# Channel gate over a 384x384x384 image: tiles of 60 rows in four slots instead of 44 rows in six, and a shorter first load

## The chip, the cores and the metric

The kernel runs on one core of a Trainium2 chip. The metric is the device time of one execution in microseconds (us). It is about 1.6 us longer than the span of the profile, which runs from the first to the last instruction.

PE is TensorE, DVE is VectorE, ACT is ScalarE, SP is SyncE, POOL is GpSimd. "Engine" alone means a compute engine; the 16 DMA engines are always called so.

## The reference, cut to what matters

```python
g = jnp.einsum("bhwc->bc", x) / (H * W)      # mean of each of 384 channels
s = sigmoid(g * w1d[0])                      # k = 1: one weight
return x * s[:, None, None, :]               # x is (1, 384, 384, 384), bfloat16
```

The gate depends on all of x, and x (113.25 MB) doesn't fit on the chip. Read plainly, this needs x twice and the output once. The kernel avoids the second reading by a guess that it checks, as follows.

## The kernel before: the parts that matter

A "row" here is 384 channels of one pixel in each of 128 partitions, 98,304 bytes; x has 1152 such rows. The kernel computes an early gate `s_early` from the first 4 rows, multiplies every tile by it and stores it, while PE sums all rows. In the end it compares the true gate with the early one, bit by bit, and would do everything again if they differed. With these inputs they agree, and that second pass isn't run.

```python
FIRST, EARLY, TILE, SLOTS, BOTH = 8, 4, 44, 6, 4
...
load(base, FIRST, 0)                              # 8 lead rows, SyncE's queue
for k in range(BOTH):                             # first tiles: half on each queue
    load(slot(k), TILE, row0(k), ("sync", "scalar"))
    if k == 0:
        plan.dma("scalar", w_one[0:1, 0:1], w1d.unsqueeze(0), writes=["w_one"])
for k in range(BOTH, SLOTS):
    load(slot(k), TILE, row0(k))                  # the others on SyncE's queue
...
for k in range(n_tiles):
    if k >= SLOTS:
        put(slot(k), TILE, row0(k - SLOTS))       # multiply in place, then store
        load(slot(k), TILE, row0(k))              # waits until that store has landed
    there = rows(slot(k), TILE)
    plan.relay(ready, "gpsimd", "tensor", there, there, ["acc1"])   # PE sums the tile
plan.signals("tensor", rows(base, FIRST), ["acc1"])
for k in range(n_tiles - SLOTS, n_tiles):
    put(slot(k), TILE, row0(k))
put(base, FIRST, 0)                               # the lead rows are stored last
```

`put` is one DVE multiply over the whole tile and one store on ScalarE's queue. The planner derives the waits: the multiply writes the tile in place, so it waits until PE has summed it. A tile's way is therefore load, landing, PE sum, DVE multiply, store, landing, and then its slot is free for another load.

## Time and profile before

| | before |
|---|---|
| device time, median | 529.16 us (529.02 to 529.28, 4 runs) |
| span of the profile | 527.6 us |
| moved by DMA | 226.53 MB, 429 GB/s |
| PE, DVE busy | 46% each |

The page of the kernel before: busy time of the engines, the DMA engines' share of each of 40 slices in tenths, and the packets.

```profile
PE 243.7 (46%) x851; PEld 0.2 (0%) x2; DVE 241.1 (46%) x45; ACT 2.7 (1%) x4; POOL 0.3 (0%) x6
...
DMA  9999999999999999999999999999999999999998
...
DMA packets 8357, 226.53 MB, mean 429 GB/s; under 512 B 930, under 2 KB 930, under 8 KB 1186
```

The 16 DMA engines are the bound: no slice but the last is below nine tenths. The Trainium skill, "DMA: Bandwidth & Descriptors", Where 436 GB/s comes from, puts the ceiling of 16 ports at 435.2 GB/s; full stretches of this trace show 433.

The chain of waits of the same kernel; its last piece (start, us, what) is the check of the guess:

```profile
515.11 0.15 DVE redo L415
```

This chain isn't what ends the run. The packet records go on until 527.1 us. The chain follows instructions, and the last stores have no instruction after them, so in a DMA-bound kernel the tail must be read from the DMA records.

The tail of the kernel before, in order of time (start us, length us, engine, line, operation, and in brackets the idle time before it and what ended it):

```profile
488.75 22.25 ACTq L109 DMA_DIRECT2D out_dram<-arena  x3
490.56 4.00 PE L238 MATMUL acc<-arena,ones 128*128 128x512 bf16 x9 [10.84 <-PEq L279]
494.78 5.19 PE L238 MATMUL acc<-arena,ones 128*128 128x512 bf16 x23 [0.22 <-issue]
...
500.01 10.63 DVE L202 TENSOR_TENSOR arena<-arena,s_early 128x16896 bf16<-128x16896 bf16 x2 [11.29 <-PE acc L238]
```

The last load landed at 489.9 us. PE summed that tile until 500.0; the first 9 matmuls took 4.00 us and the next 23 took 5.19, which fits what the Trainium skill, "TensorE: Matmul & The Clock Gate", Part 1, says of a clock that is at half speed after idling. DVE multiplied the tile (8.96 us) and then the 8 lead rows (1.75 us). The store of the tile was issued at 509.0 us.

The stretches around it (us; busy time and number of instructions of PE, PEld, DVE, ACT, POOL; granted clock; DMA share; GB/s). A packet is counted whole in the stretch in which it starts, so a share may pass 1:

```profile
500.00:505.00 5.00, 0.62 (x3) 0.00 (x0) 4.99 (x1) 0.00 (x0) 0.00 (x0) 1.00 1.00 433
505.00:510.00 5.00, 0.00 (x0) 0.00 (x0) 5.00 (x2) 0.00 (x0) 0.00 (x0) 0.51 1.02 439
510.00:515.00 5.00, 0.00 (x0) 0.00 (x0) 4.11 (x9) 0.61 (x1) 0.00 (x0) 0.50 0.99 426
515.00:520.00 5.00, 0.00 (x0) 0.00 (x0) 0.22 (x2) 0.00 (x0) 0.00 (x0) 0.50 1.00 433
```

By the packet records the first DMA engine ended the earlier stores at 513.6 us, and the last tile's packets followed at once.

DMA issues (output<-input, queue, count, KB each, median us from issue to landing), and the making of the early gate:

```profile
out_dram<-arena ACTq DMA_DIRECT2D x26, 4224.0 KB, 52.7
arena<-in_x_dram SPq DMA_DIRECT2D x22, 4224.0 KB, 48.1
```

```profile
12.60 0.16 PE L337 MATMUL w_all<-w_one,ones 1*128 1x1 bf16 x1 [12.60 <-DMA w_one<-in_w1d_dram]
...
16.93 0.61 ACT L369 ACTIVATE s_early<-total,w_scaled 128x384 bf16<-128x384 f32 x1 [12.55 <-DVE total L311]
...
26.24 17.83 DVE L202 TENSOR_TENSOR arena<-arena,s_early 128x16896 bf16<-128x16896 bf16 x2 [9.35 <-PE acc L238]
```

The gate was ready at 17.5 us, but the first multiply began at 26.24, when PE had summed the first tile. The gate wasn't what it waited for.

### The profile page before, as it was taken

What the parts mean: (1) busy time and instruction counts of PE and PEld (TensorE: products, weight loads), DVE (VectorE), ACT (ScalarE), POOL (GpSimd) and SP (SyncE); (2) the same over time, 40 slices, a digit from 0 to 9 for tenths busy, and PEclk for the clock granted to TensorE, in tenths of its full rate; (3) what the DMA queues carried; (4) which work ended last, traced back from release to release, by engine and by line L of the source; (5) the groups of instructions that cost most, each with busy time, mean ns of one, the idle gap of its engine ahead of it and who ended that gap; (6) DMA issues with size and microseconds to landing.
All of it is one profiled execution on the core that took longest, in us unless ns stands there. A gap on an engine that the chain in (4) does not pass through costs nothing. (4 is left out here: it accounts for less than half of the span.)

```text
span 527.6 us, 1093 instructions
## 1 busy us (share of the span) xinstructions
PE 243.7 (46%) x851; PEld 0.2 (0%) x2; DVE 241.1 (46%) x45; ACT 2.7 (1%) x4; POOL 0.3 (0%) x6
## 2 busy tenths in 40 slices
PE   0876561652651651652742642642733733633700
PEld 0000000000000000000000000000000000000000
DVE  0298626326336336336246336246156156156190
ACT  1000000000000000000000000000000000000000
POOL 0000000000000000000000000000000000000000
PEclk9998867866767867866757867868757768768765
DMA  9999999999999999999999999999999999999998
GB/s 384 430 429 410 428 438 436 425 446 418 443 425 441 436 425 446 418 443 420 446 433 428 443 420 443 420 446 433 428 443 420 441 423 443 436 425 446 416 443 358
DMA packets 8357, 226.53 MB, mean 429 GB/s; under 512 B 930, under 2 KB 930, under 8 KB 1186
## 3 DMA queue, kind: packets, MB, share of 16 engines
q10 hardware_dynamic: 4466, 121.90, 53.6%
q1 hardware_dynamic: 3888, 104.60, 46.2%
q8 instruction: 1, 0.02, 0.0%
q14 instruction: 2, 0.02, 0.0%
HBM read 113.25 MB, written 113.25 MB: 429 GB/s over the span
## 5 line engine op out<-in xcount | busy, mean ns | idle before, releaser
L238 PE MATMUL acc<-arena,ones 128*128 128x512 bf16 x846 | 242.6, 453 | 244.3 <-PEq L279 242.7
L202 DVE TENSOR_TENSOR arena<-arena,s_early 128x16896 bf16<-128x16896 bf16 (+1 forms) x27 | 234.5, 8691 | 259.2 <-PE acc L238 259.2
L337 PE MATMUL w_all<-w_one,ones 1*128 1x1 bf16 x1 | 0.2, 158 | 12.6 <-DMA w_one<-in_w1d_dram 12.6
L346 DVE TENSOR_SCALAR w_scaled<-w_all 128x1 f32<-128x1 f32 x2 | 0.2, 154 | 11.6 <-PE w_all L337 11.6
L311 DVE TENSOR_TENSOR total<-total,acc 128x128 f32<-128x128 f32 (+2 forms) x11 | 4.5, 408 | 0.3
L393 ACT ACTIVATE arena<-total,w_scaled 128x384 bf16<-128x384 f32 x1 | 0.6, 615 | 495.7 <-DVE total L311 495.7
L331 ACT ACT_TABLE_LOAD x1 | 1.3, 1283 | 2.9 <-issue 2.9
L309 DVE COPY total<-acc 128x384 f32<-128x384 f32 x1 | 0.6, 558 | 1.2 <-PE acc L238 1.2
L401 DVE TENSOR_TENSOR total<-arena,s_early 128x384 f32<-128x384 uint16 x1 | 0.6, 559 | 0.7 <-ACT arena L393 0.7
L238 PE MATMUL acc<-zeros,ones 128*128 128x512 bf16 x3 | 0.8, 380 | 0.0
L369 ACT ACTIVATE s_early<-total,w_scaled 128x384 bf16<-128x384 f32 x1 | 0.6, 615 | 12.5 <-DVE total L311 12.5
L355 DVE MEMSET ones<- 128x128 bf16 x1 | 0.2, 165 | 1.0 <-PEq L522 1.0
L236 PE MATMUL acc<-arena,ones 128*128 128x512 bf16 x1 | 0.6, 607 | 0.0
L409 DVE TENSOR_REDUCE wrong<-total 128x1 f32<-128x384 f32 x1 | 0.6, 553 | 0.0
L331 ACT ACTIVATE warm<-warm 128x1 f32<-128x1 f32 x1 | 0.2, 203 | 0.0
L415 DVE CAST redo<-wrong 128x1 int32<-128x1 f32 x1 | 0.2, 153 | 0.0
L236 PEld LDWEIGHTS acc<-arena,ones 128*128 128x128 bf16 x1 | 0.1, 106 | 0.0
L337 PEld LDWEIGHTS w_all<-w_one,ones 1*128 1x128 bf16 x1 | 0.1, 100 | 12.6 <-issue 12.6
L522 POOL MEMSET const-bfloat16-1.0<- 128x1 bf16 x1 | 0.1, 101 | 0.0
L522 POOL MEMSET const-uint8-127<- 128x1 uint8 x1 | 0.1, 101 | 0.0
L354 POOL MEMSET zeros<- 128x2 bf16 x1 | 0.1, 99 | 0.0
L353 POOL MEMSET warm<- 128x1 f32 x1 | 0.1, 98 | 0.5 <-POOLq L522 0.5
(2 smaller groups left out, 0.2 us busy)
## 6 DMA issues: line engine op xcount, KB each, us to landing
out_dram<-arena ACTq DMA_DIRECT2D x26, 4224.0 KB, 52.7
arena<-in_x_dram SPq DMA_DIRECT2D x22, 4224.0 KB, 48.1
arena<-in_x_dram ACTq DMA_DIRECT2D x4, 2112.0 KB, 26.0
arena<-in_x_dram SPq DMA_DIRECT2D x4, 2112.0 KB, 30.5
arena<-in_x_dram SPq DMA_DIRECT2D x1, 768.0 KB, 7.1
out_dram<-arena ACTq DMA_DIRECT2D x1, 768.0 KB, 16.8
w_one<-in_w1d_dram ACTq DMA_DIRECT2D x1, 0.0 KB
```

Source lines behind the costliest of these rows:

```text
L202: return lambda e: e.tensor_tensor(to_v, v, s_b, ALU.mult)
L236: loaded.append(e.matmul(bank, weights, moving, start=start, stop=stop))
L238: return e.add_instruction(mybir.InstMatmult(name=nc.get_next_instruction_name(), engine=mybir.EngineType.PE, ins=[e.lower_ap(moving), e.l ...
L309: emit = lambda e, part=part, of=of: e.tensor_copy(part, of)
L311: emit = lambda e, part=part, of=of: e.tensor_tensor(part, part, of, ALU.add)
L331: lambda e: e.activation(warm[:, 1:2], warm[:, 0:1], ACT_F.Sigmoid),
L337: lambda e: e.matmul(w_all[:, 0:1], ones[0:1, :], w_one[0:1, 0:1], start=True, stop=True),
L346: lambda e, i=i, n=n: e.tensor_scalar_mul(w_scaled[:, i : i + 1], w_all[:, 0:1], 1.0 / float(P * n)),
L369: lambda e: e.activation(s_early[:], total[:], ACT_F.Sigmoid, scale=w_scaled[:, 0:1]),
L393: lambda e: e.activation(s_true, total[:], ACT_F.Sigmoid, scale=w_scaled[:, 1:2]),
L401: lambda e: e.tensor_tensor(total[:], s_true.bitcast(U16), s_early[:].bitcast(U16), ALU.not_equal),
L409: lambda e: e.reduce_max(wrong[:], total[:], axis=mybir.AxisListType.X),
```

## The change

Its intent: fewer and larger transfers, and an early gate that is ready sooner. The tile has 60 rows (5760 KB a transfer), four slots hold 240 rows (before: 264), the lead tile has 12 rows, of which SyncE's queue loads 4 first; the weight is SyncE's second transfer; the other 8 lead rows come after the first tile on both queues. Only the first two tiles, not the first four, are loaded in halves on both queues.

```diff
-FIRST, EARLY, TILE, SLOTS, BOTH = 8, 4, 44, 6, 4
+FIRST, EARLY, TILE, SLOTS, BOTH = 12, 4, 60, 4, 2
...
-    load(base, FIRST, 0)
+    load(base, FIRST, 0, hi=EARLY)
+    plan.dma("sync", w_one[0:1, 0:1], w1d.unsqueeze(0), writes=["w_one"])
     for k in range(BOTH):
         load(slot(k), TILE, row0(k), ("sync", "scalar"))
         if k == 0:
-            plan.dma("scalar", w_one[0:1, 0:1], w1d.unsqueeze(0), writes=["w_one"])
+            load(base, FIRST, 0, ("sync", "scalar"), lo=EARLY)
...
-    s_true = at(slot(n_tiles), 1)
+    s_true = at(base + FIRST, 1)
...
-    ahead("sync", nc.sync, 1)
+    ahead("sync", nc.sync, 2)
```

Cut: `load` learns to load a part (`lo`, `hi`), and the second pass uses the true gate's own place, so it needs no copy.

More of the change, by code (lines that the diff above doesn't have):

```diff
@@ L205, in bass_standalone__channel_attn_eca__vision_kernel @@
     base = SLOTS * TILE
-    assert (n_rows - FIRST) % TILE == 0 and base + FIRST <= n_arena
+    assert (n_rows - FIRST) % TILE == 0 and base + FIRST < n_arena
     assert FIRST % 4 == EARLY % 4 == TILE % 4 == 0 and EARLY < FIRST
@@ L215, in row0, with load @@
         return FIRST + k * TILE
-    s_true = at(slot(n_tiles), 1)
+    s_true = at(base + FIRST, 1)
     plan = Planner(nc, "a", 70)
-    def load(place, n, r0, queues=("sync",)):
-        i = 0
-        for queue, m in zip(queues, split(n, -(-n // len(queues)))):
+    def load(place, n, r0, queues=("sync",), lo=0, hi=None):
+        i, hi = lo, hi or n
+        for queue, m in zip(queues, split(hi - lo, -(-(hi - lo) // len(queues)))):
             plan.dma(
@@ L396, in bass_standalone__channel_attn_eca__vision_kernel @@
         reads=["total", "w_scaled1"],
-        writes=["s_true"] + rows(slot(n_tiles), 1),
+        writes=["s_true"],
     )
@@ L423, in bass_standalone__channel_attn_eca__vision_kernel @@
     half, r0 = base // 2, 0
-    s_kept = at(base, 1)
-    again.op(
-        "vector",
-        lambda e: e.tensor_copy(s_kept, s_true),
-        reads=rows(slot(n_tiles), 1),
-        writes=["s_kept"],
-    )
     for k, n in enumerate(split(n_rows, half)):
@@ L435, in bass_standalone__channel_attn_eca__vision_kernel @@
             "vector",
-            gate(place, place, n, s_kept),
-            reads=["s_kept"] + rows(place, n),
+            gate(place, place, n, s_true),
+            reads=rows(place, n),
             writes=rows(place, n),
@@ L463, in ahead @@
         block[barrier:barrier] = new
-    ahead("sync", nc.sync, 1)
+    ahead("sync", nc.sync, 2)
     ahead("scalar", nc.scalar, 1)
-    plan.emit("sync", nc.sync, heads["sync"] - 1)
+    plan.emit("sync", nc.sync, heads["sync"] - 2)
     plan.emit("scalar", nc.scalar, heads["scalar"] - 1)
```

## The prediction

> **What bounds it now.** The DMA engines. The page shows them in the top tenth in nearly every slice, 226.53 MB at 429 GB/s over the 527.6 us span; PE and DVE are busy 46% each. Packet records: 16896 B take 629 ns and 33792 B take 1251 ns, so a packet costs about 7 ns plus 0.0368 ns per byte, 27 GB/s on each of 16 engines. This agrees with the Trainium skill, "DMA: Bandwidth & Descriptors", Where 436 GB/s comes from (435 GB/s for 16 ports). By the same records the engines idle only 1.3 us before and just after the first packet (which starts at 1.05 us), nothing from 20 to 520 us, and 1.0 us at the end. The chain of waits ends with the DVE check at 515 us, but stores move until 527.1 us.
>
> **What the change removes.** Data packets go from 7424 to about 5632: 1792 x 7 ns / 16 engines = 0.8 us, and 0.1 us for completion writes. The bytes don't change. The early gate is ready sooner (the weight, which ended a 12.6 us wait of PE, comes after a 4-row load instead of behind a half tile), but no store waits for it: before, it was ready at 17.5 us, the first multiply began at 26.2 us after PE's sum, and the DMA was full of loads. So that gains nothing. The short first load (8 packets of about 120 ns per engine) may leave the engines 0.3 us idle before the next descriptors.
>
> **What it adds.** A tile's time between landing and store grows. Before: last load landed 489.9, PE sum 490.6 to 500.0 (9.4 us, first matmuls at half speed), multiply 9.0 us, store issued 509.0; its queue had work until 513.8, so about 4 us were spare. After: PE about 9.4 + 12 x 0.22 = 12.1 us, DVE 8.96 x 60/44 = 12.2 us, about 26 us with hand-overs and first byte. Four slots (240 rows) hold less backlog than six (264).
>
> Steady state: a 60-row tile takes 13.6 us alone, 27.3 us when loads and stores share the engines, so a slot returns every 27.3 us; PE and DVE use under half of that. Both queues stay filled (I estimate 3 us in hand on loads), so no loss there.
>
> Tail: stepping the queues through by hand from those durations, I put the last load's data at 484 us and landing at 486 to 487 us. About 109 rows of stores are then left, enough until about 509 us. The last tile's store can move only at 512 to 513 us. So the DMA runs dry for 3 to 4.5 us before the last tile's store (13.6 us) and the 12-row store (2.7 us), all on the critical path.
>
> **Sum.** 529.2 - 0.9 (packets) + 0.3 (start) + 3.7 (dry tail) - 0.5 (engines realigned by the gap) = 531.8 us. Range 528.8 to 534.5. Chances: faster by over 2% 0.01, within 2% 0.97, slower by over 2% 0.02.
>
> **What would show it.** Right: a DMA gap of 3 to 4.5 us between 507 and 515 us; the DMA full from 20 to 500 us; 46080 B packets of about 1703 ns; DVE multiplies of 12.2 us, PE sums about 12 us; the weight landing before 6 us and s_early ready near 10 us. Wrong: no gap before the last tile's store (then 528.3 us or less), or a hole in mid-run.
>
> **What would make it wrong.** A queue phase different from my stepping: each us of backlog more or less at the last landing moves the result by a us. A lower PE clock in the tail lengthens the gap. Large packets slower per byte, or uneven sharing, would shift both.

## The result, and the profile after

| | median | runs | ratio to before | 95% interval |
|---|---|---|---|---|
| before | 529.16 us | 529.02 to 529.28 (4) | | |
| after | 532.11 us | 530.93 to 532.60 (4) | 1.0053 | 1.0035 to 1.007 |

A ratio is the mean time of one kernel's runs over that of the other's runs of the same rounds, so it isn't quite the ratio of the medians. By the 2% rule the verdict is "same", but the interval leaves no doubt that the kernel became slower by about half a per cent. The profiled run of after is its fastest, 530.93 us; this matters for the accounts below.

The page after:

```profile
PE 218.4 (41%) x854; PEld 0.2 (0%) x2; DVE 239.9 (45%) x38; ACT 2.7 (1%) x4; POOL 0.3 (0%) x6
...
DMA  9999999999999999999999999999999999999988
...
DMA packets 6340, 226.52 MB, mean 428 GB/s; under 512 B 706, under 2 KB 706, under 8 KB 1090
```

A quarter of the packets is gone and PE's matmuls take less time, yet the run didn't become shorter. The difference is in the last two slices. The tail after, in order of time:

```profile
486.91 11.68 PE L239 MATMUL acc<-arena,ones 128*128 128x512 bf16 x45 [15.88 <-PEq L280]
...
498.63 14.63 DVE L202 TENSOR_TENSOR arena<-arena,s_early 128x23040 bf16<-128x23040 bf16 x2 [15.19 <-PE acc L239]
510.82 2.81 ACTq L109 DMA_DIRECT2D out_dram<-arena  x2
```

The stretches after:

```profile
500.00:505.00 5.00, 0.00 (x0) 0.00 (x0) 5.00 (x1) 0.00 (x0) 0.00 (x0) 0.93 1.00 433
505.00:510.00 5.00, 0.00 (x0) 0.00 (x0) 5.00 (x1) 0.00 (x0) 0.00 (x0) 0.50 0.68 295
510.00:515.00 5.00, 0.00 (x0) 0.00 (x0) 4.86 (x7) 0.00 (x0) 0.00 (x0) 0.50 0.69 295
515.00:520.00 5.00, 0.00 (x0) 0.00 (x0) 2.09 (x5) 0.61 (x1) 0.00 (x0) 0.50 1.02 442
```

Between 505 and 515 us the DMA share falls from 1.00 to 0.68 and 0.69, while DVE works on the last tile. The DMA engines have nothing to do, because the only data left to store is still being multiplied. By the packet records the first DMA engine finished the earlier stores at 508.40 us and the slowest at 510.20; the last tile's store, issued at 510.82, sent its first packet at 511.66.

The transfers, and the early gate, after:

```profile
out_dram<-arena ACTq DMA_DIRECT2D x19, 5760.0 KB, 51.0
arena<-in_x_dram SPq DMA_DIRECT2D x17, 5760.0 KB, 34.1
```

```profile
5.62 0.16 PE L338 MATMUL w_all<-w_one,ones 1*128 1x1 bf16 x1 [5.62 <-DMA w_one<-in_w1d_dram]
...
9.94 0.61 ACT L371 ACTIVATE s_early<-total,w_scaled 128x384 bf16<-128x384 f32 x1 [6.22 <-DVE total L312]
```

The early gate is ready 7 us sooner and nothing uses it sooner: the first multiply starts at 35.17 us, when PE has summed a larger first tile.

```profile
35.17 36.30 DVE L202 TENSOR_TENSOR arena<-arena,s_early 128x23040 bf16<-128x23040 bf16 x3 [25.27 <-PE acc L239]
```

**The account.** The packet records give the DMA engines' idle time: at each moment 16 minus the number of packets in flight (never under 0), summed and divided by 16.

| us, mean of 16 DMA engines | before | after | difference |
|---|---|---|---|
| idle, 0 to 20 us | 1.35 | 1.15 | -0.20 |
| idle, 20 to 505 us | 0.00 | 0.00 | 0 |
| idle, hole in the tail | 0.00 | 2.76 | +2.76 |
| idle, last 4 us (the DMA engines end unevenly) | 1.02 | 0.58 | -0.45 |
| at work | 524.75 | 524.34 | -0.41 |
| after the last packet | 0.44 | 0.51 | +0.07 |
| span of the profile | 527.56 | 529.33 | +1.77 |

So in the profiled run the loss is the hole, less what fewer packets and a more even end give back. The three unprofiled runs were another 1.0 to 1.7 us slower, and no profile says where. The small terms are uncertain by about 0.2 us: over all profiled runs the time at work is 524.7 to 525.0 us with 44-row tiles and 524.1 to 524.4 us with 60-row tiles, and the idle time of the first 20 us is 1.19 to 1.35 us with the old start and 1.15 to 1.32 us with the new one, so no effect of the start is shown.

**Why the hole.** Compare what the store queue held when the last load's data was in with what the last tile needed from there. "Needed" runs to the issue of its store plus 0.85 us, the time from issue to first packet (in after 510.82 to 511.66):

| us | before | after |
|---|---|---|
| last load's data in | 488.67 | 484.70 |
| earlier stores end (first DMA engine) | 513.65 | 508.40 |
| so the queue held | 25.0 | 23.7 |
| last tile's store issued | 509.00 | 510.82 |
| so the tile needed | 21.2 | 27.0 |
| to spare | 3.8 | -3.3 |

The -3.3 us are those of the first DMA engine that ran dry. The others followed until 510.20 us, so the mean of the 16 is 2.76 us.

The queue held about the same. The tile needed 5.8 us more, because 60 rows take PE 11.7 us instead of 9.4 and DVE 12.16 instead of 8.96, one after the other. The remaining 0.3 us is mostly the landing: the last load's completion came 1.70 us after its data instead of 1.25, which in both kernels is about the time of one full packet (1702 and 1251 ns).

One thing is easily overlooked here. In after the load queue itself was empty for 9.6 us early in the run, from 68.8 to 78.4 us. The first load into a used slot was issued at 74.27 us, when the store before it had landed (73.89). In before that load was issued at 62.55 us, and the loads ahead of it lasted until 90.3. The DMA engines weren't idle in after's gap (0.00 us), because stores ran ahead, but stores that run ahead can be missing from the backlog later. Whether and by how much this shortened the 23.7 us wasn't measured. In e7 below the same event comes with a backlog of only 16.1 us.

### The profile page after: what moved, and what is told of

It is laid out like the page before. It is cut to its first block, busy times and chain, and to the rows that moved or that the text cites. A ratio compares the mean times of both kernels' runs of the same rounds, so it can differ in the third digit from the quotient of the medians. Undisturbed runs are those within 1.5% of the kernel's fastest.

```text
span 529.3 us, 1057 instructions
## 1 busy us (share of the span) xinstructions
PE 218.4 (41%) x854; PEld 0.2 (0%) x2; DVE 239.9 (45%) x38; ACT 2.7 (1%) x4; POOL 0.3 (0%) x6
## 5 line engine op out<-in xcount | busy, mean ns | idle before, releaser
L202 DVE TENSOR_TENSOR arena<-arena,s_early 128x23040 bf16<-128x23040 bf16 (+1 forms) x20 | 233.3, 11677 | 270.1 <-PE acc L239 209.6
L239 PE MATMUL acc<-arena,ones 128*128 128x512 bf16 x849 | 217.3, 420 | 275.2 <-PEq L280 259.8
L237 PE MATMUL acc<-arena,ones 128*128 128x512 bf16 x1 | 0.6, 607 | 0.0
```

Of the source, the lines that this page charges most:

```text
L202: return lambda e: e.tensor_tensor(to_v, v, s_b, ALU.mult)
L237: loaded.append(e.matmul(bank, weights, moving, start=start, stop=stop))
L239: return e.add_instruction(mybir.InstMatmult(name=nc.get_next_instruction_name(), engine=mybir.EngineType.PE, ins=[e.lower_ap(moving), e.l ...
```

## The experiments

The main theory is this hole. The rivals: the new start shifts everything; the larger packets or tiles cost time all along; the fewer rows in the slots cost time. All kernels below gave correct results. Where a hole is given for a run, it is the mean idle time of the DMA engines in the tail, as in the account.

### e1: the new start alone, on 44-row tiles

```diff
 (the changed kernel with)
-FIRST, EARLY, TILE, SLOTS, BOTH = 12, 4, 60, 4, 2
+FIRST, EARLY, TILE, SLOTS, BOTH = 8, 4, 44, 6, 4
```

> The kernel before (44-row tiles, six slots) with only the new start: 4-row first load, weight second on SyncE's queue, other 4 rows after the first tile on both queues. Main theory (the loss is a dry DMA queue in the tail, made by the larger tiles): no store waits for the early gate, so 529.2 us within 0.4, and no DMA gap after 480 us. Rival (the new start delays the first tiles and shifts everything after): about 532 us.

Measured: 529.67 us median (528.99 to 530.75, 4 runs), ratio 1.0003 (0.9988 to 1.0017), and no hole. The new start isn't the cause of the loss. But two of the four runs were over 530 us, which I hadn't expected. In the profiled one, 530.75 us, the last completion of the final store came at 528.76 us, the one before it at 527.06, and the median of the 16 at 526.00; before, these were 527.12, 526.99 and 525.93. So one DMA engine was late there. The DMA engines' idle time in the last 4 us was 2.63 us, against 1.02 before, and this 1.6 us is all that this run lost against the profiled run of before (529.12 us).

### e2: 60-row tiles with the old start

```diff
 (the changed kernel with)
-    load(base, FIRST, 0, hi=EARLY)
-    plan.dma("sync", w_one[0:1, 0:1], w1d.unsqueeze(0), writes=["w_one"])
+    load(base, FIRST, 0)
...
-            load(base, FIRST, 0, ("sync", "scalar"), lo=EARLY)
+            plan.dma("scalar", w_one[0:1, 0:1], w1d.unsqueeze(0), writes=["w_one"])
```

> 60-row tiles in four slots with the old start (12 rows in one load, weight behind half a tile). Main theory: still slower than before, 531 to 533 us, with a DMA gap of 2 to 4 us (mean of the engines) just before the last tile's store. Rival (start): about 528.5 us.

Measured: 531.45 us (530.79 to 532.54, 4 runs), ratio 1.0045 (1.003 to 1.0059), hole 2.91 us. The tiles and slots carry the loss.

### e3: the last tile in two halves

```diff
-    for k in range(n_tiles - SLOTS, n_tiles):
+    for k in range(n_tiles - SLOTS, last):
         put(slot(k), TILE, row0(k))
+    half_tile = TILE // 2
+    put_part(slot(last), half_tile, 0, row0(last))
+    put_part(slot(last), TILE - half_tile, half_tile, row0(last))
```

> The changed kernel with the last tile's multiply and store cut into two halves of 30 rows: the first store is issued about 6 us earlier, at about 505 us, before the queue runs dry near 508 us. Main theory: the gap is gone and the time is 528.3 to 529.0 us, a little under the kernel before, and the runs agree within about 0.3 us again. Rival (larger packets or fewer slots cost time all along): it stays at about 532 us.

Measured: 529.43 us (528.83 to 531.37, 6 runs), ratio 1.0006 (0.9993 to 1.002). The stretches of its profile:

```profile
505.00:510.00 5.00, 0.00 (x0) 0.00 (x0) 5.00 (x2) 0.00 (x0) 0.00 (x0) 0.50 0.99 429
510.00:515.00 5.00, 0.00 (x0) 0.00 (x0) 4.93 (x5) 0.00 (x0) 0.00 (x0) 0.50 0.99 429
```

The first half was issued at 505.4 us, and the hole is gone: 0.99 where after had 0.68. All tiles but the last, and the slots, are those of after, and nearly all of the loss is gone too. That speaks against larger tiles costing time all along. My expectation was missed in two ways: the median is about half a us too high, and the runs don't agree within 0.3 us.

### e4: the same split on the kernel before (control)

The edit is that of e3.

> Control: the kernel before with its last tile's multiply and store cut in two halves. Its queue never ran dry (last store issued at 509.0, queue busy until 513.8), so the main theory expects no gain: 529.2 us within 0.3. If splitting helps by itself (a better end, smaller last packets), it falls below 528.8 us.

Measured: 529.14 us (529.12 to 529.34, 4 runs), ratio 0.9995 (0.9979 to 1.0012). Splitting is worth nothing where the queue isn't dry.

### e5: the lead rows stored before the last tile

```diff
-        plan.relay(ready, "gpsimd", "tensor", there, there, ["acc1"])
-    plan.signals("tensor", rows(base, FIRST), ["acc1"])
+        also = rows(base, FIRST) if k == 0 else []
+        plan.relay(ready, "gpsimd", "tensor", there, there + also, ["acc1"])
+    plan.signals("tensor", [], ["acc1"])
     for k in range(n_tiles - SLOTS, n_tiles):
+        if k == last:
+            put(base, FIRST, 0)
         put(slot(k), TILE, row0(k))
-    put(base, FIRST, 0)
```

PE sums the lead rows ahead of the first tile, so the signal that PE gives after that tile can stand for them too, instead of one at the end.

> The changed kernel with the 12 lead rows multiplied and stored before the last tile instead of after it: the same work, 2.7 us of stores moved ahead of the gap. Main theory: the gap shrinks by about 2.7 us, and the time falls to 529.2 to 530.2 us. Rival: no change, about 532 us.

Measured: 528.98 us (528.37 to 531.15, 4 runs), ratio 1.0006 (0.9989 to 1.0023). The stretches:

```profile
505.00:510.00 5.00, 0.00 (x0) 0.00 (x0) 5.00 (x1) 0.00 (x0) 0.00 (x0) 0.50 0.92 394
510.00:515.00 5.00, 0.00 (x0) 0.00 (x0) 3.98 (x10) 0.61 (x1) 0.00 (x0) 0.50 1.22 523
```

The two average 1.07, against 0.685 in after; many large packets start just before 515 us, which is why one passes 1. By the packet records the DMA engines' mean idle time in the tail was 0.00 us. The work and the number of transfers are those of after; only the order of 12 rows changed. The median is a little better than expected; in the profiled run PE was done 0.5 us sooner and the last tile's store was issued at 510.32 us.

### e6 and e7: 44-row tiles in five and in four slots

```diff
-FIRST, EARLY, TILE, SLOTS, BOTH = 8, 4, 44, 6, 4
+FIRST, EARLY, TILE, SLOTS, BOTH = 8, 4, 44, 5, 4      (e6; in e7: 8, 4, 44, 4, 4)
```

> The kernel before with five slots instead of six: 220 rows of tiles, fewer than the 240 of the changed kernel. Main theory (what counts is the stores left at the last landing against the time from landing to store): with five slots a load is still issued 7 us before the load queue needs it, so the schedule is the same as with six: 529.2 us within 0.4, no gap. Rival (what costs is the number of rows that the slots hold): worse than the changed kernel, over 532 us.

Measured: 528.95 us (528.68 to 529.01, 4 runs), ratio 0.9992 (0.9976 to 1.0009), no hole. Five slots hold 220 rows, fewer than the 240 of after, and nothing is lost. So the number of rows in the slots isn't by itself the cause.

> The kernel before with four slots of 44 rows. Now a load waits for its slot, the load queue runs empty for a while, stores run ahead, and by hand about 17.5 us of stores are left at the last load's end against about 22 us until the last tile's store moves. Main theory: a gap of about 4 us in the tail and 532 to 534 us, although the packets are those of before. Rival (the larger packets or 60-row tiles cost time): 529.2 us.

Measured: 534.81 us (533.17 to 535.58, 4 runs), ratio 1.0107 (1.009 to 1.0124). The stretches of its profiled run, the fastest, with a hole of 4.01 us:

```profile
510.00:515.00 5.00, 0.00 (x0) 0.00 (x0) 5.00 (x1) 0.00 (x0) 0.00 (x0) 0.78 0.74 318
515.00:520.00 5.00, 0.00 (x0) 0.00 (x0) 4.93 (x5) 0.00 (x0) 0.00 (x0) 0.50 0.51 216
```

This is the other way into the same hole. The last load's data was in at 497.63 us and the earlier stores ended from 513.74, so the queue held 16.1 us; the store was issued at 517.31 us, so the tile needed 20.5. Here the need is that of before and the backlog is short: with four slots a load waits for its slot, the load queue empties (between 49.2 and 59.5 us no load packet moves), and stores run ahead with the whole bandwidth. It is the same event as the one at 68.8 us in after. The size was under-estimated: 534.81 against at most 534.

### e8 and e9: a useless DVE operation ahead of the last tile's multiply

```diff
     for k in range(n_tiles - SLOTS, n_tiles):
+        if k == last:
+            plan.op(
+                "vector",
+                lambda e: e.reduce_max(wrong[:], at(slot(last), 5), axis=mybir.AxisListType.X),
+                reads=rows(slot(last), TILE),
+                writes=["wrong"] + rows(slot(last), TILE),
+            )
         put(slot(k), TILE, row0(k))          (e8: 5 rows; e9: 16 rows; on the kernel before)
```

`wrong` is written anew afterwards, so the result stays right.

> As e9, with a reduction over 5 rows (about 2.1 us), less than the 3 to 3.5 us that the queue had to spare. Main theory: no gap, 529.2 us within 0.4. Rival (every us on the last tile's way to its store costs a us): 531.3 us.

Measured: the reduction took 2.15 us, and the time was 529.32 us (529.12 to 529.51, 4 runs), ratio 1.0 (0.9984 to 1.0015).

> The kernel before with one useless VectorE reduction over 16 rows put ahead of the last tile's multiply (about 6.4 us, to be read from its trace). The queue has about 3.5 us to spare there. Main theory: a gap of about 3 us opens in the tail, and the time is about 532 us. Rival: no change, 529.2 us.

Measured: the reduction took 6.55 us, and the time was 532.01 us (530.71 to 532.29, 4 runs), ratio 1.0041 (1.0025 to 1.0058), hole 3.11 us. The reductions (e8, then e9), and then the stretches in the same order:

```profile
501.04 2.15 DVE L389 TENSOR_REDUCE wrong<-arena 128x1 f32<-128x1920 bf16 x1 [11.26 <-PE acc L238]
500.81 6.55 DVE L389 TENSOR_REDUCE wrong<-arena 128x1 f32<-128x6144 bf16 x1 [11.29 <-PE acc L238]
```

```profile
510.00:515.00 5.00, 0.00 (x0) 0.00 (x0) 4.93 (x5) 0.00 (x0) 0.00 (x0) 0.50 1.00 433
515.00:520.00 5.00, 0.00 (x0) 0.00 (x0) 2.62 (x7) 0.61 (x1) 0.00 (x0) 0.50 1.00 433
```

```profile
510.00:515.00 5.00, 0.00 (x0) 0.00 (x0) 5.00 (x1) 0.00 (x0) 0.00 (x0) 0.50 0.74 318
515.00:520.00 5.00, 0.00 (x0) 0.00 (x0) 4.86 (x7) 0.00 (x0) 0.00 (x0) 0.50 0.76 324
```

This is the threshold itself. Before had 3.8 us to spare by the table; 2.15 us of delay cost nothing, 6.55 us cost 2.8 (6.55 - 3.8 = 2.75). That the sum comes out so closely is partly luck, because the spare time differs from run to run. In the profiled run of e9 the last load landed at 490.98 us, not 489.93, and without the reduction about 2.9 us would have been spare. There the first DMA engine ran dry for 3.6 us, and the mean of the 16 was 3.11. No tile or packet was changed, and the hole and the loss of after appear.

### f1, f2, f3: where does the spread come from?

Two kernels without a hole had runs well over their fastest (e1, e3), and e5 had one at 531.15 us. These runs look for the cause in the parts of the start, and try the best combination.

```diff
 (f1: the kernel before, only the weight moved)
     load(base, FIRST, 0)
+    plan.dma("sync", w_one[0:1, 0:1], w1d.unsqueeze(0), writes=["w_one"])
 (f2: e1, with the weight back behind the first half tile of ScalarE's queue)
 (f3: e2, with the reordering of e5)
```

> The three kernels so far with the new start and no gap (e1, e3, e5) had runs 1 to 2.5 us over their fastest, the kernels with the old start and no gap (before, e4, e6) hardly 0.7. Here the kernel before gets only the new place of the weight (SyncE's second transfer). If the weight's place makes the spread, some of the runs reach 530 us or more; if the split first load does, all stay within 529.0 to 529.7. Main theory for the median: 529.2 us within 0.4 either way.

Measured: 529.12 us (529.06 to 529.50, 5 runs), ratio 0.9999 (0.9986 to 1.0013).

> The kernel before with only the split first load (4 rows first, 4 after the first tile on both queues), the weight where it was. If the split load makes the spread, some of the runs reach 530 us or more; if the weight's place does, all stay within 529.0 to 529.7. Main theory for the median: 529.2 us within 0.4.

Measured: 529.05 us (528.95 to 530.15, 5 runs), ratio 1.0001 (0.9988 to 1.0015). Four runs are within 0.3 us and one is at 530.15.

> 60-row tiles in four slots, the old start, and the lead rows stored before the last tile: the candidate that may beat both. Main theory: the gap is nearly closed as in e5, fewer packets save 0.4 us, and with the old start the runs agree: 528.4 to 528.9 us, spread under 0.7 us. If the 60-row tiles and not the start make the spread, some runs reach 530 us or more.

Measured: 529.62 us (528.77 to 530.47, 5 runs), ratio 1.001 (0.9996 to 1.0023). The hole was 0.06 us, as it should be, but the expected gain didn't come, and the spread came with the old start too.

So the spread stays open. All three 60-row kernels whose hole is closed (e3, e5, f3) show it; of the 44-row kernels without a hole, e1 and one run of f2 do, and e4, e6, e8 and f1 don't. Of these six, e1 and f2 are the two whose first load is split, but one run of f2 is thin evidence. The kernels with a hole spread as well, by 1.6 to 2.4 us. A late DMA engine was seen in two profiled runs, e1 (1.7 us after the second last, idle time of the last 4 us 2.63 us) and e3 (1.1 us after, idle 2.00 us), but not why it was late. And no version clearly beats the kernel before: the best, e6, has an interval that includes 1.

## Why the prediction was right, point by point

The predicted 531.8 us stands against 532.11 measured, and the mechanism was the one named. That the two agree within 0.3 us is partly luck, as the end of this section shows.

| step, as predicted | measured |
|---|---|
| DMA-bound, and full from 20 to 500 us | idle 0.00 us from 20 to 500 us in both; right |
| both queues stay filled, 3 us in hand on loads | after's load queue was empty from 68.8 to 78.4 us; wrong, but the DMA engines stayed busy with stores |
| the early gate gains nothing | e1, f1, f2: ratios 1.0003, 0.9999, 1.0001; right |
| weight before 6 us, gate near 10 us | PE used the weight at 5.62 us, gate at 10.6 us; right |
| 46080 B packets about 1703 ns | 1702 ns; right |
| PE sum 12.1, DVE 12.2 us | 11.7 and 12.16; right |
| last load's data at 484, landing 486 to 487 us | 484.70 and 486.41; right |
| stores last until about 509 us | 508.4 to 510.2 us; right |
| the last store moves at 512 to 513 us | 511.66 us; slightly early |
| hole 3 to 4.5 us | 3.3 for the first DMA engine; mean of the 16 2.76, in e2 2.91; a little smaller |
| packets save 0.9 us | 0.41 in this pair, about 0.3 to 0.9 over other pairs; likely too much |
| start costs 0.3 us | 0.20 less in this pair, within the scatter of the runs; not seen |
| more even end gives 0.5 us | 0.45; right |

Three terms of the sum were mis-sized. The first is the saving by packets. I fitted 7 ns per packet to the durations of single packets. But records of successive packets overlap a little: in mid-run up to 18 are in flight on 16 DMA engines at once. The summed durations did fall by 1.07 us per DMA engine (526.65 to 525.59), but the time at work fell by 0.41 only, or 0.41 x 16 / 1792 = 3.7 ns for each of the 1792 packets saved. That figure is loose: with the 0.3 to 0.9 us of other pairs of runs it would be 2.7 to 8 ns. The second is the start, whose cost wasn't seen. The third is the hole, because PE was 0.4 us faster than I took it, the store began 0.85 us after its issue instead of over a us, and the DMA engines ran dry one after the other and not all at once.

In the profiled run, which took 530.93 us, these errors add up to a prediction that is 0.9 us too high. In the median run it is 0.3 us too low. So the close hit on the median contains 1.2 us between the profiled run and the median that the mechanism doesn't explain; the spread of f1 to f3 is the same open question.

## What to carry to other kernels

In this kernel, which keeps the DMA engines full, the change of tile size and slots mattered only where it left them without work. In one like it, compare the backlog of stores when the last load is in with the time that the last tile still needs to its store. If the need is larger, cut the last tile alone or move an independent store ahead of it (e3 and e5 gave back nearly all), rather than giving up the tile size. Look also at whether a load must wait for its slot early in the run, since stores that run ahead then are missing at the end. Fewer and larger transfers were worth little here (0.41 us), where the DMA engines always had work from one queue or the other, and an input that was ready sooner was worth nothing, because its first user waited for something else.

## What the Trainium skill lacked or had wrong

- "DMA: Bandwidth & Descriptors", Anatomy of one DMA, gives a fit for GpSimd's path of about 2.0 us fixed per DMA plus bytes over the rate. It doesn't give what is left of this while other transfers keep the DMA engines busy. Here 58 large transfers became 44 for the same bytes, and the DMA engines' time at work fell by 0.41 us in all.
- The same page, Why small descriptors are slow, gives about 3 cycles of fixed overhead per packet, but not of which clock. At the 850 MHz of its section Where 436 GB/s comes from, that is 3.5 ns, an estimate. Here a packet cost 7 ns by the durations of single packets (16896 B in 629 ns, 33792 B in 1251 ns), but 3.7 ns in effect in the one pair of runs, as packets overlap. This doesn't contradict the estimate, but other pairs give 2.7 to 8 ns, so it doesn't confirm it either.
- The same page, Latency and other measured facts, gives about 0.6 us to the first byte for transfers issued by SyncE or ScalarE, as all of these are. Here, with the queue dry, it was 0.84 to 0.85 us from the start of the issuing instruction to the first packet (after, e2, e7, e9); that instruction itself took 0.34 us, so about 0.5 us after its end. This is near the figure if it counts from there, which the page doesn't say.
- No page has the balance: the backlog at the last load (23.7 us after, 25.0 before) against the last tile's way to its store (27.0 and 21.2).
- "DMA: Bandwidth & Descriptors", Latency and other measured facts, says that DMA engines 7 and 15 are usually slower, and ties this, as a best guess, to transfers issued by GpSimd, of which there are none here. The records here don't number the DMA engines, so this is neither confirmed nor refuted, but what was seen is a DMA engine that ends late in some runs only: in a run of e1 the last completion came 1.7 us after the second last, in before 0.14 us after. The cause is open.
